# A scaled copy in three buffers, own weights as column tiles, transposes and gate products in one matmul, odd chunks' heads swapped, last tokens by rows

## The chip, the cores and the metric

One core of one Trainium2 chip runs the program. The metric is device time in microseconds (us), the median of the runs shown. Engine names are the profile's: PE is TensorE (PEld its weight loads), DVE VectorE, ACT ScalarE, POOL GpSimd, SP SyncE, which issues DMAs.

## The reference

Attention of the RWKV kind over 4 batches, 8 heads, 768 tokens and 48 dimensions, then one of 8 experts for each token. In full precision:

```python
for t in range(S):
    cur = np.einsum('bhd,bhe->bhde', u[None] * kt, vt)
    y[:, :, t] = np.einsum('bhd,bhde->bhe', rt, state + cur)
    state = w[None, :, :, None] * state + np.einsum('bhd,bhe->bhde', kt, vt)
x = attn_out.transpose(0, 2, 1, 3).reshape(B * S, H * D)       # 3072 x 384
expert_idx = np.argmax(x @ w_gate, axis=1)                     # 8 experts
h = np.maximum(xe @ w1[e], 0.0)                                # 384 -> 1024
out[mask] = gate_w[mask, None] * (h @ w2[e])                   # 1024 -> 384
```

## The kernel before

The program has two bodies. `straight` (lines 41 to 476) computes the whole reference with fixed sizes. `general` (485 to 929) computes the whole reference again, without those sizes and with other tiles: levels of masked scores (lines 683 to 700), 31 tiles of tokens whose expert is read into a register (855 to 928). `rwkv5_then_switch` runs `straight`, loads the integer `flag` into a register of each engine (line 938) and enters `general` under `tc.If(bad > 0)` (940).

`flag` is a sum of 13 tests (457): each expert's token count above `CAP` = 416 (453), each head pair's decays outside 0.7 to 1.4 (455, from line 159), and the count of expert 0 after three batches below `EARLY` = 256 (435).

**Attention in `straight`.** A pair is two heads of one batch, 16 pairs in all; 768 tokens are 6 chunks of 128. The order of all work is written out by hand in the loop at 399 to 437, each engine keeps it, and a dependency tracker adds the waits. In turn i:

- `prep(i+1)` (195): DVE multiplies r and k of the next pair by powers of the decay into `RKs[(i+1) % 2]` (200); POOL makes `rps` = r times k (203) and `Kds` (204).
- `p_own(i)` (207): the product of each token with itself, six matmuls of two columns into the PSUM bank `dsb`, then a copy by ACT; `diag(i)` (223) puts it on the diagonals of `A`.
- `p_scores(i)` (214): chunk products out of `RKs[i % 2]`; `mask` (228) copies the part above the diagonal into `A` on DVE.
- `p_ds(i)` (238): what each chunk adds to the state, into `dsb` too; `scan(i)` (246) runs the states on DVE.
- `p_out(i-1)` (252): first the products of `A` with v, then (265) the states with r out of `RKs[(i-1) % 2]`, into the PSUM tile `yps`; ACT copies them to `yTs` (267, 268).
- `p_tr(i-2)` (270) transposes y back to tokens by rows, in two halves; `p_lg(i-2)` (275) makes the gate's logits, six matmuls of eight columns; `keep` and `keep_lg` (280, 285) copy and add them on DVE.

After the fourth pair of a batch, `route(b)` (293) chooses experts, ranks the tokens with small matmuls and scatters each token's row by POOL's indirect DMA into `rows`, at its expert's next place (318). After the third batch the first 256 rows of expert 0 are loaded (436) and transposed (437) within the loop.

**Experts in `straight`.** Ten passes: expert 0 in 256 and 160 token places, experts 1 to 6 in 416 each, expert 7 in 256 and 160. A pass loads its rows (345), transposes them in blocks on DVE (354), multiplies by `w1` (360) and by `w2` (369), and `put` (379) scales the result and scatters it, one indirect DMA for each 32 places of a pass; 128 partitions carry four quarters of a row of 384 values, so 13 DMAs of 128 rows of 384 bytes serve 416 places. Places behind the expert's count get an index out of bounds and are not written.

## Time and profile before

| | us |
|---|---|
| median of 3 runs | 1725.42 |
| runs | 1720.04 to 1747.9 |
| profiled execution, time | 1715.44 |
| profiled execution, span from the first to the last instruction | 1713.7 |

The page gives for the profiled execution: PE busy 1476.1 us (86% of the span), PEld 1026.7 (60%), DVE 667.2 (39%), ACT 277.2 (16%), POOL 430.2 (25%); 19189 instructions; mean granted clock of PE 0.790 of full speed. A matmul of 32-bit values appears as two records. Rows name a line of the kernel, the engine, the operation, and output<-inputs; x is a count; the time in brackets is the idle time before and what ended it.

### The profile page before, as it was taken

What the parts mean: (1) busy time and instruction counts of PE and PEld (TensorE: products, weight loads), DVE (VectorE), ACT (ScalarE), POOL (GpSimd) and SP (SyncE); (2) the same over time, 40 slices, a digit from 0 to 9 for tenths busy, and PEclk for the clock granted to TensorE, in tenths of its full rate; (3) what the DMA queues carried; (4) which work ended last, traced back from release to release, by engine and by line L of the source; (5) the groups of instructions that cost most, each with busy time, mean ns of one, the idle gap of its engine ahead of it and who ended that gap; (6) DMA issues with size and microseconds to landing.
All of it is one profiled execution on the core that took longest, in us unless ns stands there. A gap on an engine that the chain in (4) does not pass through costs nothing.

```text
span 1713.7 us, 19189 instructions
## 1 busy us (share of the span) xinstructions
PE 1476.1 (86%) x7014; PEld 1026.7 (60%) x7014; DVE 667.2 (39%) x1668; ACT 277.2 (16%) x824; POOL 430.2 (25%) x533
## 2 busy tenths in 40 slices
PE   7999788888887629899889899989965998999898
PEld 6887676544444627677667676767743444544444
DVE  6455211111110166766764766665413212211211
ACT  4333211000000001213112211311110000010000
POOL 6134211122222562323330322222001111111110
PEclk9576559999998855959865755765557999999999
DMA  9355105333310054001010100100005444444440
GB/s 215 97 174 185 52 28 156 94 102 102 104 60 26 24 190 172 22 21 57 28 29 21 47 23 21 49 21 15 1 28 207 143 149 161 144 138 170 140 143 1
DMA packets 56784, 152.66 MB, mean 89 GB/s; under 512 B 33497, under 2 KB 37642, under 8 KB 49650
## 3 DMA queue, kind: packets, MB, share of 16 engines
q1 hardware_dynamic: 46706, 118.46, 22.2%
q0 software_dynamic: 8832, 20.38, 3.8%
q10 hardware_dynamic: 1152, 12.58, 2.0%
q8 instruction: 57, 0.93, 0.2%
q14 instruction: 37, 0.30, 0.1%
HBM read 131.20 MB, written 21.96 MB: 89 GB/s over the span
## 4 chain that ended last, share of the span: by engine, by line
PE 44%; issue 12%; DVE 3%; POOL 2%; ACT 1%; DMA 0%; POOLq 0%; DVEq 0%; ACTq 0%
PE sc L694 11%; PE hpg L885 7%; PE ypg L903 7%; PE sc L688 5%; PE yp L705 3%; PE dsp L658 2%; DVE Ag L696 2%; PE yp L702 2%; PE xtp L723 2%; PE lgp L726 1%; PE dsp L660 1%; PE hTp L896 1%; ACT Ag L691 1%; PE ktp L651 1%; DVE xm L873 1%
## 5 line engine op out<-in xcount | busy, mean ns | idle before, releaser
L694 PE MATMUL sc<-Rl,Kl 128*128 128x128 f32 x768 | 234.1, 408 | 17.2 <-DVE Ag L696 15.8
L696 DVE COPY_PREDICATED Ag<-masks,sc 128x128 f32<-128x128 int32 x480 | 162.5, 352 | 200.8 <-PE sc L694 195.0
L631 POOL TENSOR_TENSOR Kl<-kT,Wr 128x192 f32<-128x192 f32 x192 | 113.1, 591 | 357.6 <-PE sc L694 303.2
L694 PEld LDWEIGHTS sc<-Rl,Kl 128*128 128x128 f32 x768 | 164.5, 270 | 63.1 <-DVE Ag L696 40.8
L365 PE MATMUL X<-xT,w1s 128*128 128x416 f32 (+2 forms) x480 | 158.4, 489 | 42.7 <-DVE xT L357 19.2
L635 DVE TENSOR_TENSOR Rl<-rT,Wp 64x192 f32<-64x192 f32 x384 | 169.6, 442 | 9.3 <-PE sc L688 3.4
L885 PE MATMUL hpg<-w1g,xTg 128*128 128x512 f32 x372 | 168.5, 603 | 0.7 <-DVE xTg L877 0.7
L903 PE MATMUL ypg<-w_all,hTg 128*128 x496 | 165.1, 486 | 0.4 <-DVE hTg L897 0.4
L388 POOL DMA_INDIRECT out_dram<-yo,ix x104 | 101.2, 974 | 248.3 <-DVE yo L385 168.1
L365 PEld LDWEIGHTS X<-xT,w1s 128*128 128x128 f32 x480 | 94.0, 211 | 106.2 <-issue 52.3
L688 PE MATMUL sc<-Rl,Kl 128*32 128x64 f32 (+1 forms) x576 | 126.2, 316 | 22.4 <-ACT Ag L691 20.4
L903 PEld LDWEIGHTS ypg<-w_all,hTg 128*128 128x128 f32 x496 | 94.2, 190 | 72.5 <-issue 14.4
L906 DVE TENSOR_SCALAR yog<-ypg,xsg 128x384 f32<-128x384 f32 x31 | 19.1, 617 | 289.4 <-PE ypg L903 289.4
L691 ACT COPY Ag<-sc 32x64 f32<-32x64 f32 (+1 forms) x288 | 63.6, 221 | 362.4 <-PE sc L688 361.1
L908 POOL DMA_INDIRECT out_dram<-yog,idx x31 | 31.4, 1013 | 343.0 <-DVE yog L906 331.8
L885 PEld LDWEIGHTS hpg<-w1g,xTg 128*128 128x128 f32 x372 | 69.1, 192 | 77.0 <-issue 75.5
L376 DVE STREAM_TRANSPOSE yq<-yps 128x416 f32<-128x416 f32 (+2 forms) x20 | 10.6, 530 | 252.6 <-PE yps L374 252.6
L688 PEld LDWEIGHTS sc<-Rl,Kl 128*32 128x32 f32 (+1 forms) x576 | 55.0, 144 | 79.4 <-ACT Ag L691 40.5
L374 PE MATMUL yps<-hT,w2s 128*128 128x416 f32 (+2 forms) x320 | 96.4, 456 | 6.2 <-DVE yq L376 6.2
L887 ACT ACTIVATE hg<-hpg 128x512 f32<-128x512 f32 x62 | 37.0, 597 | 385.6 <-PE hpg L885 385.6
L374 PEld LDWEIGHTS yps<-hT,w2s 128*128 128x128 f32 x320 | 58.7, 196 | 43.1 <-issue 29.4
L367 ACT ACTIVATE hT<-X 128x416 f32<-128x416 f32 (+2 forms) x80 | 35.8, 448 | 295.1 <-PE X L365 250.1
(220 smaller groups left out, 1950.3 us busy)
## 6 DMA issues: line engine op xcount, KB each, us to landing
...
```

Source lines behind the costliest of these rows:

```text
L365: nc.tensor.matmul(p[:, 0:self.n], lhsT=w1s[self.e % 3][:, m, f * 128:(f + 1) * 128], rhs=self.t[:, m, 0:self.n], start=m == 0, stop=m == ...
L374: nc.tensor.matmul(p[:, 0:self.n], lhsT=w2s[self.e % 3][:, f, m * 128:(m + 1) * 128], rhs=self.h[:, f, 0:self.n], start=f == 0, stop=f == ...
L388: s_ = nc.gpsimd.indirect_dma_start(out=out4[:, :], out_offset=bass.IndirectOffsetOnAxis(ap=ix[:, k:k + 1], axis=0), in_=yo[:, k, :], in_o ...
L631: nc.gpsimd.tensor_tensor(levels(Kl[:, l - 1, :], l)[:, :, 0, :], levels(kh, l)[:, :, 0, :], bc(Wr[:, hp, None, C - n:C], [128, nb, n]), o ...
L635: nc.vector.tensor_tensor(Rl[q, l, hi, :].rearrange("p (b j) -> p b j", j=n), levels(rh, l)[q, :, 1, :], bc(Wp[q, hp, None, 0:n], [64, nb, ...
L688: nc.tensor.matmul(sc[s0:s0 + n, l, :, js], lhsT=Kl[:, l - 1, c * C + s0:c * C + s0 + n], rhs=Rl[:, l, :, c * C // 2 + blk * n:c * C // 2 ...
L691: nc.scalar.copy(A[s0:s0 + n, :, s0 + n:s0 + 2 * n], sc[s0:s0 + n, l, :, js])
L694: nc.tensor.matmul(sc[:, l, :, :], lhsT=lhs, rhs=Rl[:, l, :, c * C // 2:(c + 1) * C // 2], start=True, stop=True, skip_group_check=True)
L696: nc.vector.copy_predicated(A.rearrange("p h (b two j) -> p h b two j", two=2, j=n)[:, :, :, 1, :], bc(masks[:, None, l, :].bitcast(I32), ...
L705: nc.tensor.matmul(yp[:, c, hi * D:(hi + 1) * D], lhsT=A[:, hi, :], rhs=vt[:, c0 + c, hi * D:(hi + 1) * D], start=c < cr and hi == 0, stop ...
L885: nc.tensor.matmul(p, lhsT=m["xT"][:, d, :], rhs=m["w1"][:, d, fb * 512:(fb + 1) * 512], start=d == 0, stop=d == DT - 1)
L903: nc.tensor.matmul(p, lhsT=m["hT"][:, f, :], rhs=w2_all[:, ds(m["e"], 1), f * DM:(f + 1) * DM], start=f == 0, stop=f == FT - 1)
```

## The change

`RKs` gets a third buffer, and its readers and its writer go by `% 3`. `p_own` makes four matmuls, one for each 32 tokens of a chunk, with the two own weights as the loaded operand and 192 columns, and `own_t` transposes the result in blocks of 32 on DVE. `p_out` keeps even chunks in one bank of `yps` and odd chunks in the other, with the heads' partitions swapped for odd chunks; all products with `A` come first, then all with the states. `p_tr` and `p_lg` become one matmul per chunk with `sel` as the moving operand: 96 columns of the identity, in order of the chunk's parity, and 8 of the gate. `sel` is filled by POOL at the start. `route` is split into `choose`, `p_rank`, `slots`, `gates`, `total` and `send`, which stand in turns 4b+5 to 4b+8. The zero fill of `rows` moves to turn 3, weights are loaded in halves, the load of expert 0's first rows moves to turn 15 and its transpose behind the loop, and the loop is one turn shorter. The first pass's matmuls with `w1` stand between the last batch's steps. Expert 7 is split into 160 and 256 places, and its second pass multiplies tokens by rows (`tokens_out`): 2 x 8 matmuls of 384 columns, one multiply and one scatter of 128 full rows each.

```diff
-    wgs = cp.tile([KP, HP, E], FP32, name="wgs")
+    wgs = cp.tile([KP, 2, HP, E], FP32, name="wgs")
...
+    sel = cp.tile([KP, 2, HP, 2 * D + E], FP32, name="sel")
...
-    nc.gpsimd.memset(zt, 0.0)
-    nc.sync.dma_start(rows.rearrange("(e n) c -> e (n c)", e=E)[:, PAD * HP * Q:CAP * HP * Q].rearrange(
-        "e (p z) -> p e z", p=128), bc(zt[:, None, :], [128, E, nz]))
...
+    def clear():
+        nc.gpsimd.memset(zt, 0.0)
+        nc.sync.dma_start(rows.rearrange("(e n) c -> e (n c)", e=E)[:, PAD * HP * Q:CAP * HP * Q].rearrange(
+            "e (p z) -> p e z", p=128), bc(zt[:, None, :], [128, E, nz]))
...
+    for par in range(2):
+        for h in range(2):
+            o = 64 * (h ^ par)
+            nc.gpsimd.tensor_copy(sel[:, par, :, h * D:(h + 1) * D], bc(ident[0:KP, None, o:o + D], [KP, HP, D]))
+    nc.gpsimd.tensor_copy(sel[:, :, :, 2 * D:], wgs)
...
-    RKs = [ca.tile([128, 2, S], FP32, name=f"RK{i}") for i in range(2)]
+    RKs = [ca.tile([128, 2, S], FP32, name=f"RK{i}") for i in range(3)]
...
-    own = [ca.tile([128, 2 * G], FP32, name=f"own{i}") for i in range(2)]
-    yTs = [ca.tile([128, S], FP32, name=f"yT{i}") for i in range(3)]
+    own = [ca.tile([128, G, 32], FP32, name=f"own{i}") for i in range(2)]
+    yTs = [ca.tile([128, 2, S // 2], FP32, name=f"yT{i}") for i in range(3)]
...
-        nc.vector.tensor_tensor(RKs[i % 2][0:KP].rearrange("p u (c t) -> p u c t", t=C),
+        nc.vector.tensor_tensor(RKs[i % 3][0:KP].rearrange("p u (c t) -> p u c t", t=C),
...
     def p_own(i):
         hp = i % HP
-        for c in range(G):
-            nc.tensor.matmul(dsb[:, 240 + 2 * c:242 + 2 * c], lhsT=rps[i % 2][0:KP, c * C:(c + 1) * C],
-                             rhs=ubs[:, hp, :], start=True, stop=True, skip_group_check=True)
-        nc.scalar.copy(own[i % 2], dsb[:, 240:240 + 2 * G])
+        x = rps[i % 2][0:KP].rearrange("p (c a j) -> p a c j", a=4, j=32)
+        for a in range(4):
+            nc.tensor.matmul(dsb[32 * a:32 * a + 2, 240:240 + 32 * G].rearrange("p (c j) -> p c j", j=32),
+                             lhsT=ubs[:, hp, :], rhs=x[:, a], start=True, stop=True, skip_group_check=True)
+    def own_t(i):
+        nc.vector.transpose(own[i % 2].rearrange("p c m -> p (c m)"), dsb[:, 240:240 + 32 * G])
...
     def p_scores(i, cs):
-        r = RKs[i % 2]
+        r = RKs[i % 3]
...
-            nc.scalar.activation(A[:, place(c, h), :], ident, func=ACT.Copy, scale=own[i % 2][:, 2 * c + h:2 * c + h + 1])
+            nc.scalar.activation(A[:, place(c, h), :], ident, func=ACT.Copy, scale=own[i % 2][:, c, h:h + 1])
...
     def p_out(i):
-        v, A, St, r = vks[i % 4], Aw[i % 2], Ss[i % 2], RKs[i % 2]
-        for cs in (range(4), range(4, G)):
-            o = yps[:, cs[0] // 4, :]
-            for c in cs:
-                for h in range(2):
-                    nc.tensor.matmul(o[64 * h:64 * h + D, (c % 4) * C:(c % 4 + 1) * C], lhsT=v[:, c, 0, h * D:(h + 1) * D],
-                                     rhs=A[:, place(c, h), :], start=c == cs[0], stop=c == 0, skip_group_check=True)
-            for c in cs:
-                if c == 0:
-                    continue
-                for h in range(2):
-                    q = slice(64 * h, 64 * h + D)
-                    nc.tensor.matmul(o[q, (c % 4) * C:(c % 4 + 1) * C], lhsT=St[q, :, c - 1],
-                                     rhs=r[q, 0, c * C:(c + 1) * C], start=False, stop=True, skip_group_check=True)
-        nc.scalar.copy(yTs[i % 3][0:KP, 0:512], yps[0:KP, 0, :])
-        nc.scalar.copy(yTs[i % 3][0:KP, 512:S], yps[0:KP, 1, 0:S - 512])
...
-    def p_tr(i, hf):
-        for c in range(3):
-            g = 3 * hf + c
-            nc.tensor.transpose(tr[:, c * 128:c * 128 + KP], yTs[i % 3][0:KP, g * C:(g + 1) * C], ident[0:KP, 0:KP])
...
-    def p_lg(i):
...
+        v, A, St, r = vks[i % 4], Aw[i % 2], Ss[i % 2], RKs[i % 3]
+        def o(c, h):
+            p = 64 * (h ^ (c & 1))
+            return yps[p:p + D, c & 1, (c // 2) * C:(c // 2 + 1) * C]
         for c in range(G):
-            nc.tensor.matmul(tr[:, 384 + E * c:384 + E * (c + 1)], lhsT=yTs[i % 3][0:KP, c * C:(c + 1) * C],
-                             rhs=wgs[:, i % HP, :], start=True, stop=True, skip_group_check=True)
-    def keep(i, hf):
+            for h in range(2):
+                nc.tensor.matmul(o(c, h), lhsT=v[:, c, 0, h * D:(h + 1) * D], rhs=A[:, place(c, h), :],
+                                 start=c < 2, stop=c == 0, skip_group_check=True)
+        for c in range(1, G):
+            for h in range(2):
+                q = slice(64 * h, 64 * h + D)
+                nc.tensor.matmul(o(c, h), lhsT=St[q, :, c - 1], rhs=r[q, 0, c * C:(c + 1) * C],
+                                 start=False, stop=True, skip_group_check=True)
+    def out_t(i):
+        for k in range(2):
+            nc.scalar.copy(yTs[i % 3][0:KP, k], yps[0:KP, k, 0:S // 2])
+    W_ = 2 * D + E
+    trv = [tr[:, 0:4 * W_].rearrange("p (c w) -> p c w", w=W_),
+           X23[:, :, 2 * C:2 * C + W_]]
+    def p_tr(i):
+        for c in range(G):
+            nc.tensor.matmul(trv[c // 4][:, c % 4, :], lhsT=yTs[i % 3][0:KP, c & 1, (c // 2) * C:(c // 2 + 1) * C],
+                             rhs=sel[:, c & 1, i % HP, :], start=True, stop=True, skip_group_check=True)
+    def keep(i):
         b, hp = divmod(i, HP)
-        nc.vector.tensor_copy(xbs[b % 2][:, 3 * hf:3 * hf + 3, hp, 0:2 * D].rearrange("p c (h d) -> p c h d", h=2),
-                              tr[:, 0:384].rearrange("p (c h d) -> p c h d", c=3, h=2)[:, :, :, 0:D])
...
+        nc.vector.tensor_copy(xbs[b % 2][:, 0:4, hp, 0:2 * D], trv[0][:, :, 0:2 * D])
+        nc.scalar.copy(xbs[b % 2][:, 4:G, hp, 0:2 * D], trv[1][:, :, 0:2 * D])
+        for cs, t in ((slice(0, 4), trv[0]), (slice(4, G), trv[1])):
+            lg, l = lgs[b % 2][:, cs], t[:, :, 2 * D:]
+            if hp == 0:
+                nc.vector.tensor_copy(lg, l)
+            else:
+                nc.vector.tensor_tensor(lg, l, lg, op=ALU.add)
...
+        def tokens_out(self):
...
+            for t in range(nt):
+                p = ybank[t]
+                for f in range(FT):
+                    nc.tensor.matmul(p[:, 0:DM], lhsT=self.h[:, f, t * 128:(t + 1) * 128], rhs=w2s[self.e % 3][:, f, :],
+                                     start=f == 0, stop=f == FT - 1, skip_group_check=True)
+                y = yt[t]
+                nc.vector.tensor_scalar_mul(y.rearrange("p (a m i) -> p m a i", a=HP, m=DT),
+                                            p[:, 0:DM].rearrange("p (m a i) -> p m a i", a=HP, m=DT), xg[:, t, 0:1])
+                s_ = nc.gpsimd.indirect_dma_start(
+                    out=out[:, :], out_offset=bass.IndirectOffsetOnAxis(ap=it2[:, t:t + 1], axis=0),
+                    in_=y[:, :], in_offset=None, bounds_check=N - 1, oob_is_err=False)
...
+    LAST = 160
     passes = [Pass(0, 0, EARLY, 0), Pass(0, EARLY, CAP - EARLY, 1)] + [Pass(e, 0, CAP, e + 1) for e in range(1, E - 1)] + \
-             [Pass(E - 1, 0, EARLY, E), Pass(E - 1, EARLY, CAP - EARLY, E + 1)]
+             [Pass(E - 1, 0, LAST, E), Pass(E - 1, LAST, CAP - LAST, E + 1)]
+    first = passes[0]
...
     prep(0)
-    for i in range(U + 2):
-        if i < U:
+    for i in range(U + 1):
+        last = i == U
+        b, k = divmod(i - 6, 4)
+        rt = i >= 6
+        if not last:
             p_own(i)
+            own_t(i)
             p_scores(i, range(4))
-        if 2 <= i:
-            p_tr(i - 2, 0)
+        if rt and k == 0:
+            p_rank(b)
+            slots(b)
         prep(i + 1)
-        if i < U:
+        if not last:
             diag(i)
         if 2 <= i:
-            keep(i - 2, 0)
-        if i < U:
+            p_tr(i - 2)
+        if not last:
             p_ds(i)
             p_scores(i, range(4, G))
             mask(i, 0)
             mask(i, 1)
+        if 2 <= i:
+            keep(i - 2)
+        if not last:
             mask(i, 2)
             scan(i)
-        if 2 <= i:
-            p_tr(i - 2, 1)
-            p_lg(i - 2)
-        if 1 <= i <= U:
+        if rt and k < 3:
+            if k == 0:
+                gates(b)
+                total(b)
+            m = 3 if b == B - 2 else 2
+            send(b, range(m * k, min(m * k + m, G)))
+        if 1 <= i:
             p_out(i - 1)
-        if 2 <= i:
-            keep(i - 2, 1)
-            keep_lg(i - 2)
+            out_t(i - 1)
+        if i % 4 == 1 and i > 4:
+            choose((i - 5) // 4)
         if i % 4 == 0 and i < U:
             ids(i // 4)
         load(i + 3)
-        if i in (6, 10):
-            weights((i - 6) // 4)
-        if i >= 5 and i % 4 == 1:
-            b = (i - 5) // 4
-            route(b)
-            if b == 2:
-                count(cnt3)
-                nc.vector.tensor_scalar(out=viol[:, 12:13], in0=cnt3[:, 0:1], scalar1=float(EARLY), scalar2=None, op0=ALU.is_lt)
-                passes[0].load()
-                passes[0].xT()
+        if i == 3:
+            clear()
+        if i in (6, 9):
+            weights(0, (i - 6) // 3)
+        if i in (13, 14):
+            weights(1, i - 13)
+        if i == 14:
+            count(cnt3)
+            nc.vector.tensor_scalar(out=viol[:, 12:13], in0=cnt3[:, 0:1], scalar1=float(EARLY), scalar2=None, op0=ALU.is_lt)
+        if i == U - 1:
+            first.load()
+    first.xT()
+    first.L1(range(0, 1))
+    p_tr(U - 1)
+    keep(U - 1)
+    choose(B - 1)
+    first.L1(range(1, 5))
+    p_rank(B - 1)
+    slots(B - 1)
+    gates(B - 1)
+    total(B - 1)
+    send(B - 1, range(G))
+    first.L1(range(5, FT))
...
-    for q in passes[1:3]:
-        q.load()
+    passes[1].load()
+    passes[2].load()
+    passes[-1].load_ids()
...
+    for k in range(2, n):
+        p = passes[k]
+        if k == n - 1:
+            passes[k - 1].L2()
+            passes[k - 1].put()
+        p.xT()
+        p.L1()
+        if k < n - 1:
+            passes[k - 1].L2()
         if k + 1 < n:
             passes[k + 1].load()
-        passes[k - 1].put()
-        if k < n and passes[k].e + 2 < E and passes[k].e != passes[k - 1].e and passes[k].e + 2 > 2:
-            weights(passes[k].e + 2)
+        if k < n - 1:
+            passes[k - 1].put()
+            if 1 < p.e + 2 < E and p.e > 0:
+                weights(p.e + 2)
+    passes[-1].tokens_out()
```

Not shown: the split of `route` line for line, the tiles of `tokens_out`, new columns of `tr` for counts, and the host's second arrangement of the gate's weights.

## Rows read from the trace of the kernel before

**Rows 1.** The page's chain of work that ended last, by line.

```profile
PE sc L694 11%; PE hpg L885 7%; PE ypg L903 7%; PE sc L688 5%; PE yp L705 3%; PE dsp L658 2%; DVE Ag L696 2%; PE yp L702 2%; PE xtp L723 2%; PE lgp L726 1%; PE dsp L660 1%; PE hTp L896 1%; ACT Ag L691 1%; PE ktp L651 1%; DVE xm L873 1%
```

**Rows 2.** Instructions on the tile flag: min/median/max ns, first and last start.

```profile
L938 POOLq TENSOR_LOAD <-flag x1: 507/507/507, 597.3 to 597.3; - x1
```

**Rows 3.** Stretches: length; busy us (count) by engine; clock, DMA share, GB/s.

```profile
10.10:51.40 41.30, 39.78 (x392) 34.67 (x392) 23.71 (x28) 16.86 (x56) 21.76 (x13) 0.88 0.78 182
51.40:211.80 160.40, 147.09 (x1322) 124.53 (x1320) 70.89 (x128) 51.53 (x168) 48.70 (x40) 0.64 0.46 135
...
245.90:272.20 26.30, 23.46 (x104) 19.05 (x102) 3.43 (x15) 3.07 (x8) 5.87 (x6) 0.95 0.63 200
272.20:473.90 201.70, 176.09 (x528) 96.52 (x528) 25.63 (x58) 23.13 (x48) 50.88 (x53) 0.97 0.34 101
473.90:515.60 41.70, 36.28 (x96) 18.66 (x96) 4.89 (x11) 4.14 (x8) 12.51 (x14) 0.95 0.16 48
515.60:605.60 90.00, 62.31 (x240) 47.29 (x240) 9.37 (x26) 5.51 (x16) 37.85 (x39) 0.82 0.09 26
605.60:1713.70 1108.10, 960.16 (x4131) 660.31 (x4131) 513.95 (x1356) 164.56 (x498) 245.54 (x345) 0.77 0.24 83
```

**Rows 4.** Timeline: start, duration, engine, line; idle time before and its releaser.

```profile
605.64 0.06 DVE L509 MEMSET wug<- 128x4 f32 x1 [10.58 <-DMA out_dram<-yo,ix]
```

**Rows 5.** POOL's DMA queue (packets, MB, share), 322 to 366, then 408 to 451.

```profile
q0 software_dynamic: 416, 0.57, 4.5%
...
q0 software_dynamic: 416, 0.64, 5.0%
```

**Rows 6.** Timeline around turn 9: a write and a read of the tile RK.

```profile
116.94 1.74 DVE L200 TENSOR_TENSOR RK<-rk,TT 112x1536 f32<-112x1536 f32 x1
...
125.71 0.90 PE L265 MATMUL yps<-RK,S 48*48 48x128 f32 x12
```

**Rows 7.** Stretches as in rows 3: two turns.

```profile
118.80:127.90 9.10, 9.10 (x127) 7.96 (x126) 4.58 (x12) 4.71 (x16) 0.00 (x0) 1.00 0.52 131
78.60:94.70 16.10, 16.10 (x126) 13.74 (x123) 9.60 (x16) 4.70 (x16) 12.12 (x10) 0.50 0.48 147
```

**Rows 8.** Timeline within the turn at clock 1.00, PE.

```profile
118.81 1.50 PE L210 MATMUL dsb<-ubs,rp 112*128 112x2 f32 x12
...
121.33 0.51 PE L273 MATMUL tr<-ident,yT 112*128 112x112 f32 x3
...
123.35 1.42 PE L277 MATMUL tr<-wgs,yT 112*128 112x8 f32 x12
```

**Rows 9.** Stretches within both turns: p_out at 1.00; own, gates, p_out at 0.50.

```profile
124.70:127.90 3.20, 3.20 (x52) 2.54 (x52) 2.25 (x9) 0.06 (x1) 0.00 (x0) 1.00 0.04 9
...
78.60:81.30 2.70, 2.70 (x21) 2.68 (x18) 1.61 (x8) 0.92 (x3) 0.41 (x1) 0.50 0.93 301
...
86.70:89.30 2.60, 2.60 (x14) 2.58 (x13) 0.00 (x0) 0.00 (x0) 2.28 (x3) 0.50 0.45 165
89.30:94.70 5.40, 5.40 (x46) 3.90 (x45) 4.90 (x5) 0.00 (x0) 5.25 (x4) 0.50 0.08 29
```

**Rows 10.** Groups by line and form, DVE: busy us, mean ns, idle before.

```profile
L232 DVE COPY_PREDICATED A<-strict,X 128x512 f32<-128x512 int32 x32 | 21.9, 722 | 2.7 <-PE X L220 2.5
...
L248 DVE TENSOR_TENSOR_SCAN S<-dec,dsb 112x240 f32<-112x240 f32 x16 | 10.1, 634 | 0.0
...
L357 DVE STREAM_TRANSPOSE xT<-xs 128x160 f32<-128x160 f32 x6 | 1.6, 315 | 0.1
```

**Rows 11.** Timeline, DVE in turn 13.

```profile
200.17 1.10 DVE L357 STREAM_TRANSPOSE xT<-xs 128x256 f32<-128x256 f32 x3 [12.59 <-DMA xs<-rows]
```

**Rows 12.** Timeline, POOL at the start.

```profile
13.58 3.40 POOL L203 TENSOR_TENSOR rp<-rk 112x768 f32<-112x768 f32 x1 [2.53 <-DMA rk<-in_rk_dram]
16.94 1.20 POOL L204 TENSOR_TENSOR Kd<-vk,T 128x480 f32<-128x480 f32 x1
```

**Rows 13.** Timeline, the last step of the program on DVE.

```profile
1709.00 0.62 DVE L906 TENSOR_SCALAR yog<-ypg,xsg 128x384 f32<-128x384 f32 x1 [4.92 <-PE ypg L903]
```

More of the change, by code (lines that the diff above doesn't have):

```diff
@@ L114, in straight @@
     pos = cp.tile([128, CAP // 32], FP32, name="pos")
+    pos2 = cp.tile([128, 4], FP32, name="pos2")
     it = cp.tile([128, 64], I32, name="it")
@@ L296, in route, with choose @@
+    full = [128, G, E]
+    def choose(b):
+        lg, oh = lgs[b % 2], ohs[b % 2]
         nc.vector.tensor_reduce(mx, lg, axis=AX, op=ALU.max)
@@ L310, in route, with slots, gates @@
                              skip_group_check=True)
+    def slots(b):
+        oh, xb = ohs[b % 2], xbs[b % 2]
+        nc.vector.tensor_tensor(rko, rp, oh, op=ALU.mult)
+        with nc.allow_low_precision("whole numbers below 2^24"):
+            nc.vector.tensor_reduce(slot[b % 2], rko, axis=AX, op=ALU.add)
+    def gates(b):
+        xb = xbs[b % 2]
         nc.vector.tensor_reduce(se, ex, axis=AX, op=ALU.add)
@@ L331, in count, with weights @@
     def count(dst):
-        nc.tensor.matmul(tr[:, 64:64 + E], lhsT=ones, rhs=osum, start=True, stop=True, skip_group_check=True)
-        nc.vector.tensor_tensor(dst, tr[:, 64:64 + E], basef, op=ALU.subtract)
-    def weights(e):
-        nc.sync.dma_start(w1s[e % 3], w1[e])
-        nc.sync.dma_start(w2s[e % 3], w2[e])
+        nc.tensor.matmul(tr[:, 480:480 + E], lhsT=ones, rhs=osum, start=True, stop=True, skip_group_check=True)
+        nc.vector.tensor_tensor(dst, tr[:, 480:480 + E], basef, op=ALU.subtract)
+    def weights(e, which=None):
+        if which in (None, 0):
+            nc.sync.dma_start(w1s[e % 3], w1[e])
+        if which in (None, 1):
+            nc.sync.dma_start(w2s[e % 3], w2[e])
     class Pass:
@@ L358, in xT, with L1 @@
                                     self.x[:, 0:self.g, 32 * m:32 * m + 32])
-        def L1(self):
+        def L1(self, fs=range(FT)):
             h = self.h = hTs[self.k % len(hTs)]
-            for f in range(FT):
+            for f in fs:
                 p = hbank[f % 4]
@@ L367, in L1, with L2 @@
                 nc.scalar.activation(h[:, f, 0:self.n], p[:, 0:self.n], func=ACT.Relu)
-        def L2(self):
+        def L2(self, ms=range(DT)):
             y = self.y = yqs[self.k % len(yqs)]
-            for m in range(DT):
+            for m in ms:
                 p = ybank[m]
@@ L377, in L2, with load_ids @@
                                     p[:, 0:self.n].rearrange("p (g j) -> p g j", j=32))
+        def load_ids(self):
+            nt = self.n // 128
+            nc.sync.dma_start(xg[:, 0:nt], rows[self.e * N + self.s0:self.e * N + self.s0 + self.n, 2 * D:Q].rearrange(
+                "(t p) c -> p t c", p=128))
+        def tokens_out(self):
+            nt = self.n // 128
+            nc.vector.tensor_scalar(out=vt[:, 0:nt], in0=pos2[:, 0:nt], scalar1=float(self.s0), scalar2=cnt[:, self.e:self.e + 1],
+                                    op0=ALU.add, op1=ALU.is_lt)
+            nc.vector.memset(it2, 1 << 20)
+            nc.vector.tensor_scalar(out=ia[:, 0:nt], in0=xg[:, 0:nt, 1].bitcast(I32), scalar1=2, scalar2=None,
+                                    op0=ALU.logical_shift_right)
+            nc.vector.copy_predicated(it2[:, 0:nt], vt[:, 0:nt], ia[:, 0:nt])
+            for t in range(nt):
[9 more added lines that the diff above has]
+                    in_=y[:, :], in_offset=None, bounds_check=N - 1, oob_is_err=False)
+                tc.declare_no_dep(s_.ins, group="sc", reason="each token stands in one row")
+                tc.add_to_no_dep_group("sc", s_.ins)
         def put(self):
@@ L513, in general @@
     nc.vector.memset(wgs, 0.0)
-    nc.sync.dma_start(wgs[0:KP], wg)
+    nc.sync.dma_start(wgs[0:KP], wg[:, 0])
     att = ExitStack()
@@ L963, in _layout @@
         ub[q, :, h] = uh[:, h].T
-        wg[q] = gh[:, h].transpose(1, 0, 2)
+        wg[q, 0] = gh[:, h].transpose(1, 0, 2)
+        wg[64 * (1 - h):64 * (1 - h) + D, 1] = gh[:, h].transpose(1, 0, 2)
     w1 = x["moe_w1"].reshape(E, HP, DT, 32, F).transpose(0, 1, 3, 2, 4).reshape(E, 128, DT, F)
```

49 lines of the change are left out of this document (20 added, 29 removed).

## The prediction

> **What bounds the kernel now.** I read the page's chain of work by line first, to see whose lines they are [rows 1]. The reader is to see lines 688, 694, 702 and 705 on it, with 885 and 903: all of them stand in `general`, none in `straight`. The kernel has two bodies: `straight` computes everything, adds up a flag, and only when the flag is above zero does line 940 run `general`, which computes everything once more. So the next views are the flag's instructions and the stages. The last engine loads the flag at 597.3 us [rows 2]; by stages [rows 3] `straight` runs to 605.6 us, where the general path's first memset has waited 10.58 us for `straight`'s last scatter [rows 4], and 1713.7 - 605.6 = **1108.1 us are the general path**.
>
> **Why the flag is up.** It has three sources: an expert with more than CAP = 416 tokens, fewer than EARLY = 256 tokens of expert 0 in three batches, a decay outside 0.7 to 1.4. The reference on its own inputs gives 380, 348, 359, 410, 409, 389, 374, 403 tokens, 293 for expert 0 after three batches, and decays from 0.850 to 0.950: none would raise it. The trace shows other counts. `put` scatters 13 x 128 = 1664 rows of 384 bytes for an expert, and rows behind the count are sent out of bounds; the DMA queue that carries them [rows 5] moved 0.57 MB for expert 1 and 0.64 for expert 3. 348 and 410 tokens in four quarters would be 0.53 and 0.63 MB; 0.64 MB is all 1664 rows, so expert 3 had 416 tokens or more.
>
> The program text says where they come from. `prep(i+1)` stands before `p_out(i-1)` in turn i, and both use `RKs[(i+1) % 2]`: the product of state and r takes the r of pair i+2 wherever there is one. The trace has that order: the write for pair 10 at 116.94 us, the product of pair 8 out of the same buffer at 125.71 us [rows 6]. I worked the reference through with this one replacement: 373, 370, 358, **421**, 385, 365, 389, 411 tokens, 290 early. That is 0.57 MB for expert 1 and 0.64 (cut at 1664 rows) for expert 3, as in the trace, and 421 > 416 is the only source that fires. With three buffers the write goes to `(i+1) % 3` and the reader has `(i-1) % 3`: the counts are the reference's, the largest is 410, the flag is zero, and `general` does not run. This first line of the change is worth 1108 us; the rest moves the 605.6 us.
>
> **The change, part by part, against the profiled execution** (span 1713.7, time 1715.4, so 1.7 us lie around it; the median of the three runs, 1725.4, is 0.6% above).
>
> *Attention, turn by turn.* PE is busy for 147.1 us of the 160.4 from 51.4 to 211.8 [rows 3]. A turn takes 9.1 us where the granted clock is 1.00 (2.4 GHz) and 16.1 us at 0.50 (1.2 GHz) [rows 7]. The eleven turns of that stretch, less the stall of 12.59 us below, average (160.4 - 12.6) / 11 = 13.4 us: 39% of the way from the slow to the fast turn.
>
> - Own weights: 12 records of two columns, 1.50 us fast and 2.7 slow [rows 8, 9], as long as the 128-column weight loads take. Now 8 records of 192 columns with two-column weights. One column of a record costs 36.28 us / 96 / 416 = 0.91 ns in the expert stage [rows 3], so a record is 0.17 us: 1.4 us if they run one after another, 0.35 if four column tiles run at once. No row has 32-column tiles; 0.6 (fast) and 1.2 (slow) is nearer to side by side, since the two-column-tile product of `p_out` runs its 44 records of 128 columns in 3.2 us [rows 9], 0.073 each, against 0.116 by that price. Gain 0.9 and 1.5.
> - Transposes and gate products: 6 and 12 records, 2 x 0.51 + 1.42 = 2.4 us fast; slow 2.6 for the gates and, at the same ratio, 1.8 for the transposes [rows 8, 9]. Now 12 records of 104 columns with the gate's weight width: no less than 1.42, at most 1.42 + 12 x 0.095 = 2.6 fast; 2.6 to 4.7 slow. I take 1.6 and 2.9, as 104 columns (0.095) are shorter than the 0.118 that a gate record takes for its weights. Gain 0.8 and 1.5.
> - Swapped heads of odd chunks: the state products of neighbouring chunks use other quarters of the array and other banks. Bounds: nothing, or the 20 state records' half share of 3.2 and 5.4 us; I take 0.3 and 0.4.
>
> PE then has 7.1 us fast, 12.7 slow. VectorE now has the block transpose of the own weights (192 columns; the expert stage's of 160 take 0.315 us [rows 10], so 0.34), the scaled copy 1.74 [rows 6], three masks of 0.72 and the scan 0.63 [rows 10], the kept rows and gates about 0.9: 5.8 us. PE's next own product waits for that scan, so with 0.6 us of PE and the handovers the ring is about 7.6 us: that is the fast turn. At the same 39%, **a turn is 12.7 - 0.39 x 5.1 = 10.7 us**.
>
> *The stall.* VectorE waits 12.59 us in one turn for expert 0's rows [rows 11], with masks and scan behind it. The load moves to turn 15 and the transpose behind the loop: gone, with up to 4 us returning there if the scatters land late.
>
> *The start.* Five copies into `sel` stand on GpSimd ahead of the first `rp`; the last reads `wgs`, whose DMA is queued behind the second pair's loads. These land between 13.6 us and 16.9 [rows 12], so the first own product, at 10.1 us now [rows 3], comes no later than 16.9 + 0.2 + 3.4 = 20.5; I take 17.5. The zero fill, 1.2 MB ahead of pair 3's loads, goes behind. Then four turns of about 9 us (clock 0.88 there [rows 3]): 53.5. Twelve of 10.7: 181.9. The last turn has six transposes and one `p_out`, 7.5 with waits: **189.4 us, against 245.9**.
>
> *Experts.* The 26.3 us to the second pass become 28.9, since pair 15's transposes and routing now lie between the first matmuls; the scatters and the load of the second pass stay covered by the 11 us of `first.L2`. 201.7 and 41.7 us stay as they are [rows 3]: same matmuls, same order. From 515.6 us on there are 59,904 columns before (240 records) and as many after (160 + 416 + 160 + 256 columns x 48 and 384 x 32): 54 us by the price above, where the trace needs 90 with the scatters. I leave 10 us for half clock and late ScalarE (bounds 0 and 20), and after it what the same three steps cost at the end of `general`, multiply, scatter, landing: 1713.7 - 1709.0 = 4.7 us [rows 13] for thirteen scatters in a row before. The skipped branch is in no row: a flag load of 0.5 us [rows 2] at least, 10 us at most, taken as 2.
>
> Sum: 189.4 + 28.9 + 201.7 + 41.7 + 54 + 10 + 4.7 + 2 = 532.4, plus 1.7: **534 us**.
>
> *A rule beside it.* The trace shows overlapping column tiles in `p_out` only. The Trainium skill, TensorEngine Tiling, Tiling Modes (Key Properties), has different tiles load weights and multiply in parallel, and a drain at each change of mode. By it the own product is 0.35 us, some 6 us less over sixteen turns, 528 in all; a turn has fewer mode changes than before. No run here shows the drain.
>
> **Rivals.**
> 1. *The slow clock stays and the tiles do not overlap*: turns keep 13.4 us, 12 x 2.7 = 32 us more: 566; with the upper bounds of start, experts and branch up to 585. For it: 0.50 over much of the attention; against: fewer weight loads in each turn.
> 2. *VectorE's ring sets all turns*: sixteen of 7.6, t = 145 at the first expert: 490. For it: 1.00 in the fast turn, where PE is busy all the time; against: once PE waits in every turn, nothing shows that the clock holds.
> 3. *The flag stays up* by a source that I misread; 410 is only 6 under the limit. Then 1108.1 us stay and no branch is skipped: 530.4 + 1108.1 + 1.7 = 1640. The general path begins when `straight`'s last scatter lands, so this rival is no faster than before from one point on: `straight` ending later than 605.6 - 34.5 = 571 us, that is rival 1's turns under it. Against: one replacement gives both traffic figures.
>
> **Numbers.** Main case 0.68 (510 to 560), rival 1 0.14, rival 2 0.12, rival 3 0.06 (0.05 of it faster). The range 485 to 585 takes in rivals 1 and 2 and leaves out rival 3 and the joint extremes of start, stall and branch. A change under 2% can hardly be told from none here: faster by more 0.98, within 0.015, slower 0.005.
>
> **What would show it.** No instruction of lines that now stand in `general` beyond the flag's loads; the queue's traffic for expert 3 at 0.63 MB; turns of 10 to 11 us with own products under 1.3; first expert matmul near 190; no wait on expert 0's rows above 4 us; one multiply, scatter and landing at the end. Rows of `sc` in the trace would make it wrong by 1100 us; turns of 13 or of 7.6 by some 40.

## The result, and the profile after

| | us |
|---|---|
| kernel before, beside the changed one (4 runs) | 1736.6 (1720.04 to 1747.9) |
| changed kernel, median of 4 runs | **518.1** (514.95 to 519.09) |
| ratio, 95% interval | 0.3004 (0.2981 to 0.3028) |
| profiled execution of the changed kernel: time, span | 518.24, 516.4 |

Some executions of one program run at a lower granted clock and take longer (the kernel before, in one later session: 1712.9 us at a mean clock of 0.786, 1738.1 at 0.766); ratios and their intervals leave these out, medians and ranges of times keep them.

Forecast: 534 us, 485 to 585. Now the views of the changed kernel that answer to those shown of before. The last instructions on the tile `flag` (its load is line 1042 now; [rows 2]), and the page's chain of work by line [rows 1]:

```profile
L1042 DVEq TENSOR_LOAD <-flag x1: 545/545/545, 509.3 to 509.3; - x1
L1042 POOLq TENSOR_LOAD <-flag x1: 504/504/504, 509.9 to 509.9; - x1
```

```profile
PE X L403 30%; PE yps L412 16%; PE dsb L412 8%; PE X L239 4%; PE yps L282 4%; PE tr L300 3%; PE yps L435 2%; ACT hT L405 2%; DVE A L251 2%; PE yps L287 2%; DVE yo L452 2%; PE dsb L227 2%; ACT A L245 1%; PE dsb L262 1%
```

Every line on the chain stands in `straight` (its lines end before 589 now); nothing of `general` runs. POOL's DMA queue while expert 3's rows go out (345 to 388 us), as in [rows 5]: 0.63 MB, the 410 tokens of the reference, and no longer 0.64.

```profile
q0 software_dynamic: 416, 0.63, 4.7%
```

The stages, with columns as in [rows 3]: four turns, the other turns to the first expert matmul, to the second pass, five full passes, one more, the last stretch.

```profile
17.60:47.00 29.40, 25.92 (x368) 20.96 (x372) 24.08 (x30) 17.27 (x56) 19.73 (x14) 1.00 0.67 161
47.00:158.10 111.10, 97.60 (x1374) 81.24 (x1374) 74.83 (x151) 57.67 (x185) 54.89 (x40) 0.86 0.69 206
158.10:186.30 28.20, 25.35 (x131) 21.24 (x130) 7.28 (x30) 4.77 (x13) 5.90 (x6) 1.00 0.37 96
186.30:388.60 202.30, 176.63 (x520) 95.98 (x519) 24.57 (x53) 22.82 (x47) 51.96 (x53) 0.96 0.38 114
388.60:430.10 41.50, 36.25 (x99) 18.78 (x98) 4.63 (x11) 4.14 (x8) 12.48 (x14) 0.96 0.12 40
430.10:516.40 86.30, 58.09 (x223) 40.72 (x221) 8.22 (x23) 5.38 (x16) 31.91 (x33) 0.86 0.09 27
```

| term of the sum | predicted | measured | difference |
|---|---|---|---|
| to the first own product | 17.5 | 17.6 | +0.1 |
| four turns | 36 | 29.4 | -6.6 |
| twelve turns and the last | 128.4 + 7.5 | 111.1 | -24.8 |
| to the second pass | 28.9 | 28.2 | -0.7 |
| five passes, one more | 201.7 + 41.7 | 202.3 + 41.5 | +0.4 |
| last stretch | 54 + 10 + 4.7 + 2 | 86.3 | +15.6 |
| sum | 532.4 | 516.4 | -16.0 |

The turns and the last stretch are off, and they pull against each other. A turn at clock 1.00, some rows of the timeline (start, duration, engine, line; idle time before and its releaser), beside [rows 7 to 10]:

```profile
46.97 0.51 PE L227 MATMUL dsb<-rp,ubs 112*2 112x192 f32 x8 [0.70 <-DVE S L267]
47.54 0.38 DVE L231 STREAM_TRANSPOSE own<-dsb 128x192 f32<-128x192 f32 x1 [0.72 <-PE dsb L227]
47.64 1.81 POOL L217 TENSOR_TENSOR rp<-rk 112x768 f32<-112x768 f32 x1 [2.68 <-PE dsb L227]
47.84 3.23 DVE L214 TENSOR_TENSOR RK<-rk,TT 112x1536 f32<-112x1536 f32 x1
48.50 1.14 PE L300 MATMUL tr<-sel,yT 112*128 112x104 f32 x8
49.47 0.61 PE L300 MATMUL X<-sel,yT 112*128 112x104 f32 x4
51.24 1.52 PE L282 MATMUL yps<-A,vk 128*48 128x128 f32 x24
52.69 0.90 PE L287 MATMUL yps<-RK,S 48*48 48x128 f32 x20
...
54.27 0.34 PE L227 MATMUL dsb<-rp,ubs 112*2 112x192 f32 x4 [0.68 <-DVE S L267]
```

The view ends within the last row; the whole product has eight records and takes 0.51 us again. The own product takes 0.51 us (1.50 before), transposes and gates 1.6 (2.4), the output product 2.35 (3.2). Three stretches: this turn, one in which PE never waits, and a later one behind a wait:

```profile
47.00:54.30 7.30, 6.62 (x112) 5.52 (x116) 6.58 (x9) 4.66 (x16) 3.14 (x2) 1.00 1.03 273
74.92:81.47 6.55, 6.55 (x111) 5.49 (x109) 5.29 (x9) 4.68 (x15) 5.96 (x4) 1.00 1.04 280
93.50:106.00 12.50, 12.11 (x119) 10.07 (x123) 6.73 (x16) 3.93 (x13) 5.04 (x5) 0.51 0.39 95
```

There are two kinds of fast turn. Those of 7.3 us have PE waiting 0.7 us for VectorE's scan, and VectorE's scaled copy takes 3.2 us in them, at the same time as POOL's `rp` (three turns, from 32 to 54 us). In the four turns of 6.55 us PE does not wait. In the turn of the second stretch the copy takes 1.72 us, and POOL's product comes behind it:

```profile
75.80 1.72 DVE L214 TENSOR_TENSOR RK<-rk,TT 112x1536 f32<-112x1536 f32 x1
...
78.38 1.84 POOL L217 TENSOR_TENSOR rp<-rk 112x768 f32<-112x768 f32 x1
```

The clock is 1.00 in the turns up to 81 us, in those with PE's waits of 0.7 us too. Then PE waits 5.4 us (30 to 158 us, PE's waits: total, times, longest) and the next turn runs at 0.51:

```profile
PE dsb L227 <- POOL rp L217: 5.4, 1, 5.4
PE dsb L227 <- DVE S L267: 4.2, 4, 2.2
```

In the last stretch PE idles twice for ScalarE's relu (PE, then ACT). The 24 records of the first row end at 438 us, and two relus of what they made start 3 and 7 us later; the second idle time, 8.57 us, ends at 488.6.

```profile
434.44 3.53 PE L403 MATMUL X<-xT,w1s 128*128 128x160 f32 x24 [0.45 <-issue]
445.69 1.97 PE L403 MATMUL X<-xT,w1s 128*128 128x160 f32 x6 [7.72 <-ACT hT L405]
```

```profile
441.10 0.30 ACT L405 ACTIVATE hT<-X 128x160 f32<-128x160 f32 x1 [2.56 <-remote]
445.34 0.30 ACT L405 ACTIVATE hT<-X 128x160 f32<-128x160 f32 x1 [3.94 <-remote]
```

### The profile page after: what moved, and what is told of

It reads as the page before. It is cut to its first block, busy times and chain, and to the rows that moved or that the text cites. A ratio compares the mean times of both kernels' runs of the same rounds, so it can differ in the third digit from the quotient of the medians.

```text
span 516.4 us, 6947 instructions
## 1 busy us (share of the span) xinstructions
PE 420.8 (81%) x2707; PEld 279.6 (54%) x2707; DVE 152.5 (30%) x327; ACT 113.8 (22%) x326; POOL 186.1 (36%) x189
## 4 chain that ended last, share of the span: by engine, by line
PE 72%; DVE 10%; issue 9%; ACT 3%; POOL 2%; another core or an unknown queue 1%; DMA 1%; DVEq 0%; POOLq 0%; ACTq 0%
PE X L403 30%; PE yps L412 16%; PE dsb L412 8%; PE X L239 4%; PE yps L282 4%; PE tr L300 3%; PE yps L435 2%; ACT hT L405 2%; DVE A L251 2%; PE yps L287 2%; DVE yo L452 2%; PE dsb L227 2%; ACT A L245 1%; PE dsb L262 1%
## 5 line engine op out<-in xcount | busy, mean ns | idle before, releaser
L412 PEld LDWEIGHTS yps<-hT,w2s 128*128 128x128 f32 x288 | 51.7, 193 | 41.5 <-issue 30.1
L245 ACT ACTIVATE A<-ident,own 128x128 f32<-128x128 f32 x192 | 57.9, 388 | 25.1 <-DVE own L231 24.7
L357 POOL DMA_INDIRECT rows<-xb,slot x24 | 28.9, 1206 | 49.7 <-DVE osum L353 44.2
L412 PE MATMUL dsb<-hT,w2s 128*128 128x416 f32 (+2 forms) x144 | 42.8, 450 | 0.0
L214 DVE TENSOR_TENSOR RK<-rk,TT 112x1536 f32<-112x1536 f32 x16 | 38.1, 2378 | 0.0
L217 POOL TENSOR_TENSOR rp<-rk 112x768 f32<-112x768 f32 x16 | 32.1, 2008 | 13.7 <-PE X L239 6.5
L239 PE MATMUL X<-RK 48*128 48x128 f32 x384 | 35.7, 323 | 1.0 <-issue 1.0
L412 PEld LDWEIGHTS dsb<-hT,w2s 128*128 128x128 f32 x144 | 25.7, 190 | 15.7 <-issue 15.3
L239 PEld LDWEIGHTS X<-RK 48*128 48x128 f32 x384 | 28.6, 216 | 8.5 <-issue 7.5
L282 PE MATMUL yps<-A,vk 128*48 128x128 f32 x384 | 29.6, 309 | 1.5 <-issue 1.5
L282 PEld LDWEIGHTS yps<-A,vk 128*48 128x48 f32 x384 | 24.4, 141 | 4.7 <-issue 2.9
```

The costliest lines, as they stand in the source:

```text
L214: nc.vector.tensor_tensor(RKs[i % 3][0:KP].rearrange("p u (c t) -> p u c t", t=C), x[0:KP].rearrange("p u (c t) -> p u c t", t=C), bc(TT[: ...
L217: nc.gpsimd.tensor_tensor(rps[i % 2][0:KP], x[0:KP, 0], x[0:KP, 1], op=ALU.mult)
L239: nc.tensor.matmul(o, lhsT=r[q, 1, c * C:(c + 1) * C], rhs=r[q, 0, c * C:(c + 1) * C], start=True, stop=True, skip_group_check=True)
L245: nc.scalar.activation(A[:, place(c, h), :], ident, func=ACT.Copy, scale=own[i % 2][:, c, h:h + 1])
L282: nc.tensor.matmul(o(c, h), lhsT=v[:, c, 0, h * D:(h + 1) * D], rhs=A[:, place(c, h), :], start=c < 2, stop=c == 0, skip_group_check=True)
L357: s_ = nc.gpsimd.indirect_dma_start(out=rows[:, :], out_offset=bass.IndirectOffsetOnAxis(ap=slot[b % 2][:, c:c + 1], axis=0), in_=xbs[b % ...
```

## The experiments

Three groups: the flag, the parts of the attention, and what still holds up the turns. They ran in later sessions, on three chips; the records do not say whether the first session's chip is one of them. Runs of the kernel before stood beside them, with medians of 1706 to 1719 us. The last kernel of the third group ran in a session of its own. I name the kernels by what was edited.

**The third buffer alone, in the kernel before.**

```diff
-    RKs = [ca.tile([128, 2, S], FP32, name=f"RK{i}") for i in range(2)]
+    RKs = [ca.tile([128, 2, S], FP32, name=f"RK{i}") for i in range(3)]
```

with `% 3` in `prep`, `p_scores` and `p_out`.

> The kernel before with nothing changed but the third buffer of `RKs` (writer and both readers go by `% 3`). Theory, that the state product's wrong r raises the flag: no instruction of `general` runs but the flag's loads, `straight` ends where it ended, at 605.6 us, and with 2 us for the branch and 1.7 around the span the time is 609 us (600 to 620); the queue's traffic for expert 3 falls from 0.64 to 0.63 MB and for expert 1 from 0.57 to 0.53. Rival, that another test raises the flag: `general` runs as before, 1715 to 1740 us.

Measured: 596.15 us (4 runs), ratio 0.3441 (0.3411 to 0.3471). `general` is gone; its page's chain begins so, and POOL's queue for expert 1 (328 to 372 us) and expert 3 (414 to 455) carries the reference's counts (348 and 410 tokens in four quarters are 0.535 and 0.630 MB):

```profile
PE X L365 24%; PE yps L374 13%; PE yps L258 7%; PE dsb L374 7%; PE tr L277 6%; PE X L220 6%; PE yps L265 6%; PE dsb L210 4%; PE tr L273 3%; POOL out_dram L388 3%; PE dsb L243 2%; DVE RK L200 2%; DVE yo L385 2%; ACT hT L367 1%; DVE yq L376 1%
```

```profile
q0 software_dynamic: 416, 0.54, 4.2%
...
q0 software_dynamic: 416, 0.63, 5.2%
```

**Two buffers, other order, in the kernel before.**

```diff
             p_tr(i - 2, 0)
-        prep(i + 1)
...
             p_out(i - 1)
+        prep(i + 1)
```

> The kernel before with two buffers, but `prep(i+1)` moved behind `p_out(i-1)` in the turn, so that the state product reads its own r. It separates the value read from the number of buffers. Theory, that it is the order of the overwrite alone: the flag is zero here too and `general` does not run; the scaled copy (1.74 us) now waits for the state product and the next scores wait for the copy, 1 to 4 us in each of 16 turns, so 625 to 675 us. Rival, that the third buffer does something else: `general` stays, above 1715 us.

Measured: 627.28 us (one run). `general` is gone here too. So it is the order of write and read, and the third buffer buys what the order costs otherwise: some 31 us, 2 us a turn, by one run.

**Two buffers again, in the changed kernel.**

```diff
-    RKs = [ca.tile([128, 2, S], FP32, name=f"RK{i}") for i in range(3)]
+    RKs = [ca.tile([128, 2, S], FP32, name=f"RK{i}") for i in range(2)]
```

with `% 2` in the same three places.

> The changed kernel with `RKs` back at two buffers (writer and both readers go by `% 2`), all other parts of the change kept; its state product then takes r of the pair two further on. Theory: the flag rises and the 1108.1 us of `general` return: 518 + 1108 = 1626 us (1615 to 1645). Rival, that another part of the change (the routing in pieces, the gate's columns in `sel`, the moved zero fill) put the flag down: 518 us. In either case `straight` itself should be as long as in the changed kernel, within 5 us.

Measured: 1600.27 us (one run); `general` is back on its chain of work:

```profile
PE sc L798 12%; PE X L403 9%; PE hpg L989 9%; PE ypg L1007 8%; PE sc L792 6%; PE yps L412 5%; PE yp L809 3%; PE dsb L412 3%; PE dsp L762 2%; DVE Ag L800 2%; PE yp L806 2%; PE xtp L827 2%; PE lgp L830 1%; PE hTp L1000 1%; PE dsp L764 1%
```

The theory of the flag held, though the time is 15 us under its range: 1600.3 - 1108.1 = 492 and not 518, and no late relu was in its trace. That led to the repeat.

**The changed kernel, repeated.** No edit; it ran in two of the groups.

> The changed kernel once more, beside the next three. Its last stretch had two stalls that I had not priced (PE idle 7.7 and 8.6 us while ScalarE's relu, line 405, starts late although its matmul has ended); the changed kernel with two `RKs` buffers shows none there. Theory, that the stalls are not in the program: they can be missing here too, and the time is then 16 us less than 518, about 500 us (492 to 506). Rival, that the third buffer or the skipped branch makes them: they are here in every run, 515 to 519 us.

> The changed kernel a third time, beside the next three. If the two late relus of the last stretch belong to a chip and not to the program, the time is near 492 us without them (488 to 496) or near 518 with them, and the three kernels beside it show them or not with it.

Measured: 491.6 us (489.18 to 494.9), a little under the 492 to 506 of the theory, and 491.54 us (487.86 to 494.35), 26.5 us under the first session, on two chips. The last stretch of the first repeat takes 67.7 us, where it took 86.3 there and I had summed 70.7; it has no such idle time:

```profile
421.70:489.40 67.70, 54.48 (x224) 38.64 (x224) 8.65 (x25) 5.51 (x16) 32.42 (x33) 0.95 0.12 34
```

Of the 27.0 us between the two spans 18.6 lie there, 4.9 in the turns, 3.5 elsewhere. It is one program, so the late relus come from something outside it, the chip or its surroundings; what it is stays open.

**Old own product.** Six matmuls of two columns and ScalarE's copy, as in the kernel before.

```diff
-        for a in range(4):
-            nc.tensor.matmul(dsb[32 * a:32 * a + 2, 240:240 + 32 * G].rearrange("p (c j) -> p c j", j=32),
-                             lhsT=ubs[:, hp, :], rhs=x[:, a], start=True, stop=True, skip_group_check=True)
+        for c in range(G):
+            nc.tensor.matmul(dsb[:, 240 + 2 * c:242 + 2 * c], lhsT=rps[i % 2][0:KP, c * C:(c + 1) * C],
+                             rhs=ubs[:, hp, :], start=True, stop=True, skip_group_check=True)
...
-        nc.vector.transpose(own[i % 2].rearrange("p c m -> p (c m)"), dsb[:, 240:240 + 32 * G])
+        nc.scalar.copy(own[i % 2], dsb[:, 240:240 + 2 * G])
...
```

Not shown: the tile `own` and its reader `diag`, back as they were.

> The changed kernel with the own weights as before: six matmuls of two columns (12 records) and ScalarE's copy in place of four matmuls of 192 columns on column tiles and the block transpose. Theory, price of the instructions alone: the own product takes 1.5 us at clock 1.00 in place of 0.52, so 16 x 1.0 = 16 us more than the changed kernel, less up to 6 us because VectorE loses its 0.38 us transpose: +10 to +18. Rival, the clock: the tiles are what lets PE keep a granted clock of 1.00; without them the clock is 0.50 for half of the turns and these take 3 to 6 us longer: +30 to +60.

Measured: 513.31 us (508.8 to 517.4), 21.7 more than the repeat beside it. The two shorter runs, 508.8 and 509.75, are 17.2 and 18.2 us over it, at the upper end of the theory's range; the two longer ones, 25 to 26 over it, lie between theory and rival. Four stretches of it: an own product, the rest of its turn, the turn after, and a fast turn.

```profile
35.60:37.10 1.50, 1.50 (x16) 1.48 (x14) 1.37 (x1) 0.86 (x2) 0.00 (x0) 1.00 0.91 261
37.10:46.20 9.10, 9.10 (x101) 7.96 (x100) 3.73 (x8) 4.10 (x14) 3.39 (x3) 0.62 0.35 89
46.20:56.90 10.70, 10.70 (x115) 9.68 (x113) 5.10 (x8) 4.96 (x16) 3.25 (x3) 0.68 0.41 113
67.50:75.00 7.50, 7.50 (x114) 6.79 (x112) 5.46 (x11) 4.96 (x16) 3.13 (x2) 1.00 0.65 162
```

At clock 1.00 the turn is 7.5 us, with PE busy without a gap, against 6.55 and 7.3 with column tiles: in turns of 7.3 us the longer product takes the place of PE's waits and costs 0.2 us, in those of 6.55 its whole 1.0. But the 1.50 us of two-column records run at 1.00, and the clock then falls, with PE busy all the time: 10 of the 15 turns between own products take 10.6 us or a little longer (up to 11.05). A PE without pause is not enough for that, since the turns of 6.55 us have none either. 10 x 3.3 = 33 us is the rival's price; some of it comes back, since the repeat's three turns of 9.7 to 12.7 us, slow at or behind waits, are gone. The profiled execution is the longest of its four (517.4 us). It shows the rival's mechanism; how many turns were slow in the shorter three no trace shows, and there the net price is about the theory's.

**Transposes and gate products apart again.**

```diff
-            nc.tensor.matmul(trv[c // 4][:, c % 4, :], lhsT=yTs[i % 3][0:KP, c & 1, (c // 2) * C:(c // 2 + 1) * C],
-                             rhs=sel[:, c & 1, i % HP, :], start=True, stop=True, skip_group_check=True)
+            for q in (slice(0, 2 * D), slice(2 * D, W_)):
+                nc.tensor.matmul(trv[c // 4][:, c % 4, q], lhsT=yTs[i % 3][0:KP, c & 1, (c // 2) * C:(c // 2 + 1) * C],
+                                 rhs=sel[:, c & 1, i % HP, q], start=True, stop=True, skip_group_check=True)
```

> The changed kernel with each of the six matmuls against `sel` split in two, 96 columns of the identity and 8 of the gate, into the same places. Theory, price alone: 12 more records whose weights take 0.118 us each, 1.4 us a turn at clock 1.00, 16 turns: +20 us (15 to 25) over the changed kernel. Rival, the clock: with these records the granted clock falls to 0.50 for half of the turns: +35 to +65. Rival, hidden: VectorE's chain sets the turn and the records fit beside it: under +5.

Measured: 498.99 us (495.96 to 503.4), 7.4 more than the repeat, nearest to the second rival's "under +5". From the first own product to the first expert matmul, the repeat and then this kernel:

```profile
16.10:151.70 135.60, 118.34 (x1738) 98.27 (x1738) 98.64 (x180) 75.68 (x242) 74.74 (x54) 0.92 0.71 204
```

```profile
17.00:158.70 141.70, 135.75 (x1918) 117.71 (x1918) 103.74 (x181) 75.95 (x240) 73.01 (x54) 0.94 0.69 195
```

PE has 17.4 us more work, near the 20 expected, but 11 of them fill time in which it waited. The mean clock, 0.94 for 0.92, does not fall, so the first rival is out; but it is not untouched: the turn from 39.7 to 49.1 us has a mean of 0.82 with PE busy throughout, where most others take 7.8 us at 1.00.

**Heads not swapped.**

```diff
-            p = 64 * (h ^ (c & 1))
+            p = 64 * h
...
```

Not shown: `sel` and its gate columns, filled to match.

> The changed kernel without the swap of the heads of odd chunks (head h always in partitions 64h; `sel` and the gate's copy to match); the two banks and the order, all products with A and then all with the states, stay. Theory, that the swap lets a chunk's state products run beside the next one's: the state products take 0.90 us with the swap and up to 1.4 without, 0.3 to 0.5 us a turn, +5 to +8 us over the changed kernel. Rival, that the order and the banks did it and the swap is free: within 2 us of it.

Measured: 493.42 us (490.75 to 496.15): 1.8 more, with ranges that overlap, so not told apart; the rival's "within 2 us" holds and the theory's 5 to 8 does not. The state products themselves, 30 to 158 us, in the repeat and without the swap (busy us, mean ns):

```profile
L287 PE MATMUL yps<-RK,S 48*48 48x128 f32 x320 | 15.0, 293 | 0.0
```

```profile
L288 PE MATMUL yps<-RK,S 48*48 48x128 f32 x320 | 22.0, 283 | 0.0
```

7.0 us over 16 turns, 0.44 each: the swap does on PE what the theory says, and where PE waits the waits swallow it. The turns of 7.3 us stay at 7.3; those of 6.55, in which PE does not wait, become 6.99 (three of four; the fourth, 7.3).

**What holds up the turns: weights late, gate first, both.**

```diff
+    nc.sync.dma_start(wgs, wg)
     load(1)
-    nc.sync.dma_start(wgs, wg)
...
-        if i in (6, 9):
-            weights(0, (i - 6) // 3)
         if i in (13, 14):
-            weights(1, i - 13)
+            weights(0, i - 13)
...
             first.load()
+            weights(1)
```

The first two changed lines are the gate's weights, ahead of the second pair; the rest is expert weights late.

> The changed kernel with expert 0's weights loaded in turns 13 and 14, in place of 6 and 9, and expert 1's behind the loop: two transfers of 1.5 MB fewer in the queue ahead of the pairs' loads. In the repeat of the changed kernel the turns that begin at 79.6 and 91.5 us take 11.9 and 12.7 us and not 7: POOL waits for pair 10's rows, PE 5.3 us for POOL, and then the granted clock is 0.50 for 13.7 us. Theory, that these transfers delay the loads: the wait goes and the half clock behind it too, -10 us (-6 to -14). Rival, that the pairs' own bytes set the pace (DMA share 0.91 in the turns before): the wait moves to another turn, under 3 us.

> The changed kernel with the gate's weights loaded ahead of the second pair, not behind it. GpSimd waits 5.5 to 7.1 us for them at the head of its work, and the first own product is at 16.1 to 17.6 us in place of 10.1 in the kernel before. Theory, that this transfer sets the start: first own product near 10.5 us, the time 5 us shorter (-4 to -7). Rival, that the loads of the next pairs set the pace of the first turns anyway: the first product moves, the wait appears before the third or fourth turn, the time within 2 us.

> Both of the last two edits, as a faster version of the changed kernel. Theory: they add up, -15 us (-10 to -20), about 476 us where the changed kernel takes 492. Rival, that the pairs' bytes bound the attention (1.2 MB a pair): one takes from the other, -6 to -9 us.

Measured: 490.7, 490.23 and 488.59 us, beside 491.54: -0.8, -1.3 and -3.0. The rivals were nearer each time, and the ranges of all three (484.4 to 494.3) overlap the repeat's, so none is told apart from no change. The first own product did move, to 12.3 us. With the weights late the wait shrank but stayed, and its row now names another releaser. POOL, in the first repeat and then with the weights late:

```profile
89.48 0.19 POOL L364 IOTA xb<- 128x24 int32 x1 [6.45 <-DMA vk<-in_vk_dram]
89.67 1.80 POOL L217 TENSOR_TENSOR rp<-rk 112x768 f32<-112x768 f32 x1
```

```profile
89.13 0.19 POOL L364 IOTA xb<- 128x24 int32 x1 [4.46 <-DMA rows<-xb,slot]
```

The waiting instruction is an iota of 0.19 us that writes token numbers into `xb` for batch 2, while batch 0's scatters still read that buffer. By the second row it waits for their landing, and in the repeat the load of `vk` came still later; `rp` stands behind it on POOL and PE's own product behind `rp`.

**Token numbers three turns later**, on top of both edits.

```diff
-        if i % 4 == 0 and i < U:
+        if i % 4 == 3:
             ids(i // 4)
```

> The last kernel (gate's weights first, expert weights late) with one more edit: GpSimd writes a batch's token numbers in turn 4b+3 and not 4b. In turn 8 that small iota waits 4.4 us (6.5 in the changed kernel) for the landing of the scatters that read the same buffer, with the pair product `rp` behind it in GpSimd's queue and PE's own product behind that; PE idles 3.3 us (5.3), and the granted clock is 0.50 for the 13.7 us after. Theory, that this wait is the cause of both slow turns: they take 7 us each and not 9.9 and 12.6, the clock stays at 1.00 through them, and the wait of 1.9 us in turn 12 goes too: 488.6 - 8 to - 11, 478 to 481 us. Rival, that the clock falls near 90 us whatever PE waits for: only the 3.3 us go, 485 us.

Measured: **479.64 us** (6 runs, 476.93 to 486.52; ratio 0.2820, 0.2802 to 0.2838), 9 us under the kernel without it (488.59, 484.38 to 489.95; ratio 0.2879, 0.2834 to 0.2924), and the fastest of all here. The two ran in different sessions on different chips, and ranges and intervals touch, so the traces have to carry it: from the first to the last own product they show 121.4 us without and 111.9 with the edit. The same two turns without and with the edit:

```profile
78.20:100.70 22.50, 18.82 (x225) 15.53 (x223) 12.94 (x30) 9.61 (x31) 10.27 (x9) 0.70 0.48 127
```

```profile
77.10:93.00 15.90, 13.54 (x225) 11.28 (x223) 14.65 (x27) 9.60 (x31) 8.90 (x7) 1.00 0.62 178
```

6.6 us fewer for two turns, and the clock stays at 1.00: it had fallen because PE stood. The Trainium skill, TensorE: Matmul & The Clock Gate, HAM oscillation, has the clock fall when matmuls wait for data between bursts; this pair of runs agrees. Not all is gained: the two turns take 6.55 and 9.4 us, not 7 each, with 2.4 us of waits in the second, and the last turn, 8.1 us without the edit, now takes 12.6 at a mean clock of 0.73, with 2.3 us of waits.

## Why the prediction was right, and where it was not

- **The flag: right, with its cause.** One replacement explained both traffic figures, and three runs show it from both sides: the third buffer alone takes 1119 us off, the order alone 1088, two buffers bring `general` back. Rival 3 is out. The third buffer alone came to 596 and not 609 us; its last stretch takes 78 us for the 90.0 of [rows 3] and has no late relus.
- **The start: right in place (17.6 us), worth little.** Moved forward to 12.3 us, by 3.8 and 4.4 against the two repeats, it gave 1.3, which is not clear of the spread.
- **The prices of the PE edits: two right, one too low.** Own product 0.51 us for 0.6; transposes and gates 1.6 for 1.6. The output product fell by 0.85 us, from 3.2 to 2.35, where I took 0.3: the swap gives 0.44, and the rest, which stays without the swap (2.8 us there), comes with the banks or with the new order, all products with `A` and then all with the states; no run separates these two, and the order had no price in my sum. Eight records of the own product take 0.51 us, where 0.17 each, one after another, would be 1.4: the column tiles overlap. By the Trainium skill, TensorEngine Tiling (Array Packing), Tiling Modes (Key Properties), different tiles multiply in parallel; the trace agrees.
- **The turn: wrong, 8.4 us for 10.7.** The mean over turns 4 to 14 is (139.0 - 47.0) / 11. The step that failed is "At the same 39%": I took the share of slow clock as a property of the stretch. It hangs on the work in the turn, and of the parts put back on the old own product above all. With that, ten of fifteen turns are slow, and the mean from turn 4 on is 9.7 us; without it the turns at a low clock in this trace (0.51 and 0.65) stand behind PE's waits of 5.4 and 2.2 us. That the slow turns there take 10.6 us, near my 10.7, is chance, since mine was a mean of slow and fast ones. The fast turn is rival 2's only in part: VectorE's ring (7.3 us for 7.6) sets the turns in which its copy runs beside POOL's product, and PE the others, with 6.55 for the 7.1 that I summed. My argument against rival 2, that nothing shows the clock to hold where PE waits in every turn, was no evidence: it held through waits of 0.7 us. Rival 1 is out, in turns and in tiles.
- **The experts: right** within 1 us in three terms.
- **The last stretch: mis-sized**, 86.3 us for 70.7, in the term of 10 us for half clock and late ScalarE. What is left of the stretch beside the 54 us of columns and the 7.2 behind the last matmul (6.7 forecast, branch included) is 25. The late relus alone hold PE up for 7.7 and 8.6 us, where the trace of before had 5.8 and 4.2. Without them the stretch is 67.7, and the term 6.
- So 534 for 518 rests on -31 and +16, and that 518 lies in the main case's 510 to 560 is luck. Where the late relus are missing the turns alone decide, and the time, 492 us, is outside the main case, though within the range. It is near rival 2's 490, and that is partly chance too: the first expert matmul comes at 151.7 us and not at 145, and the stretches behind it are 5.3 us shorter than summed.
